# Issuing a round's loads ahead of the feed-forward stretch, and ordering the row halves of early chunks on TensorE itself

## The chip, the cores and the metric

One core of a Trainium2 chip runs the whole program. The metric is the device time of one execution in microseconds (us), the median of three executions. "PE" is TensorE's matmul stream, "PEld" its weight loads, "DVE" VectorE, "ACT" ScalarE, "POOL" GpSimd, and "SP" the engine whose queue issues nearly all transfers here.

## What is computed

A retention layer feeds a feed-forward layer with a squared ReLU:

```
scores = (q @ k.T) / sqrt(64)                 # q, k, v: 8 batches, 8 heads, 576 positions, 64 wide
attn   = (scores * gamma_h ** (i - j), i >= j) @ v
x      = attn as 4608 tokens x 512
out    = relu(x @ w_in) ** 2 @ w_out          # w_in 512 x 2048, w_out 2048 x 512
```

The decay is a power of a constant for each head, so it can be put into q and v by rows: q of position i is multiplied by gamma^i, v of position j by gamma^-j. What remains are plain products with a causal mask, and a running sum U = sum of k v^T that carries everything before the current piece.

## The kernel before

**Chunks.** Each batch of 576 positions is cut into chunks of 128, 128, 128, 128 and 64 positions, 40 chunks in all (`chunks`, `N_CH`). A chunk is worked in halves of 64 positions. For each half TensorE makes the scores (`score`, L449), which VectorE masks (`masked`, L461), the half's own contribution "own" (L480 or L568: masked scores times v), the growth of U, "grow" (L483 or L562), and the contribution of the past (L515 or L604: U times q). Own and past are added up in the same PSUM tile `x_ps`. All of these are products with 64 contraction rows: some use rows 0 to 63 of the array, some rows 64 to 127, and both kinds write the same places of `x_ps`. [...]

**How that order is made.** In the first ten chunks (`retain_a`, `retain_b`, `retain_c`), `retain_b` ends with a tiny ScalarE copy (L518, 128 x 2 elements of `x_ps` into a spare `u_sb`). It must wait for the products of `retain_b`, and the next products into `x_ps`, those of `retain_c`, must wait for it. The later chunks (`whole`) do without: their `wait_for` puts a no-operation on TensorE that waits for an earlier product's semaphore, and what shares a row half with the earlier products goes ahead of that wait.

**Rounds.** The main loop runs over i, 0 to 40. A round works chunk i - 1, prepares chunk i and then issues a stretch of the feed-forward layer (`ffn`). Up to i = 10 (`N_ONE`) a round is `retain_a`, some feed-forward work, `retain_b`, `scores`, `retain_c`, more feed-forward work. From i = 11 (`N_TURN`) on it is `whole(i - 1)` and then one stretch `ffn(i - 1, 2)`.

**Feed-forward.** The first layer goes over nine blocks of 512 tokens. Each block is four groups (`mp`) of seven products in a seven-product block scheme (`PRODUCTS`, `ffn_in`): a step is eight 128 x 128 x 256 matmuls (L708), and VectorE and ScalarE combine its result (L718 to L735) before the PSUM bank can be used again. The results g go out to a scratch tensor in DRAM (`g_sums`, store at L650). The second layer (L1038) reads them back after the attention part is over and runs to the end of the program.

**Loads and flips.** `load(i)` fetches q, k and v of a chunk: three transfers each for q and k, one for v. The pools `ld3`, `ld5` and `ld4` hold three q, five k and four v. q and k are needed transposed. Up to chunk 10 TensorE does that (`turn`); from chunk 11 on VectorE transposes blocks of 32 (`flip`, L396; k first, then q), and ScalarE moves them into place (`move`, L411). `flip(i + 2)` puts the two transposes into a list, and the stretch of feed-forward that follows takes one per step. q must first be scaled by POOL (`scale_q`, L375).

**Order.** Everything is written out by hand: `manual_schedule` keeps the program order on every engine, so on SP too transfers are issued strictly as the code names them, and one that has to wait holds back what is behind it. In the rounds up to 9 a round's loads fetch chunk i + 3. At i = 10 the loads turn to a longer lead: q and k of chunk 13, q and k of chunk 14, v of chunk 13; from there on q and k of chunk i + 4, v of chunk i + 3. All these loads stand at the end of the round (L921 to L929), behind its feed-forward stretch. The round i = 10 has one stretch more than the others, `ffn(i, 0)` at L918, ahead of its loads. The first flip of a chunk that was loaded at i = 10 is `flip(13)`, in the stretch of round 11.

Of the kernel before, what the change touches and what calls it, by code (L numbers as in the profile page):

```python
# [15 lines left out]
C = 128  # L16
CH = C // 2
# [23 lines left out]
def kernel(  # L41
# [315 lines left out]
    def rows(half, n=64):  # L357
        return slice(64 * half, 64 * half + n)
# [7 lines left out]
    def clears(half, bank):  # L366

        new = (half, bank) not in clean
        clean.add((half, bank))
        return new  # L370
# [100 lines left out]
    def x_at(hp, b, h):  # L471
        return xp[0][rows(b), hp // 2, 0:256].rearrange("p (g t) -> p g t", g=2)[:, hp % 2, CH * h:CH * h + CH]

    def within(i, h):

        s = st[i]
        b_, ci, c0, cs = chunks[i]
        own, grow = [], []
        for hp, e, b in HEADS:
            own.append(lambda hp=hp, e=e, b=b: nc.tensor.matmul(  # L480
                x_at(hp, b, h), lhsT=s["vs"][rows(h), 2 * hp + b, :], rhs=s["ret"][rows(h), e, hp, :],
                start=clears(b, hp // 2), stop=False, skip_group_check=True))
            grow.append(lambda hp=hp, e=e, b=b: nc.tensor.matmul(  # L483
                u_ps[0][rows(e), hp, :], lhsT=loaded[i][1][rows(1 - h), 2 * hp + e, :], rhs=s["vs"][rows(1 - h), 2 * hp + b, :],
                start=(ci == 0 and h == 1 and hp == 0), stop=(hp == HP - 1), skip_group_check=True))
        return own, grow
# [19 lines left out]
    def retain_b(i):  # L506

        s = st[i]
        b_, ci, c0, cs = chunks[i]
        for h in reversed(range(cs // CH)):  # L510
            if 2 * ci + h == 0:
                continue
            u = u_sb[(2 * ci + h) % 3]
            for hp, e, b in HEADS[0:2] + HEADS[4:6] + HEADS[2:4] + HEADS[6:8]:
                nc.tensor.matmul(x_at(hp, b, h), lhsT=u[rows(e), hp, :], rhs=s["qT"][rows(e), hp, CH * h:CH * h + CH],  # L515
                                 start=clears(b, hp // 2), stop=False, skip_group_check=True)

        nc.scalar.copy(u_sb[(2 * ci + (cs // CH)) % 3][:, 0:2, 0:1], xp[0][:, :, cs - CH:cs - CH + 1])  # L518

    def retain_c(i):  # L520

        b_, ci, c0, cs = chunks[i]
        own, grow = within(i, 0)
        more = ci + 1 < NCH
        for j in range(0, len(own), 2):
            for f in own[j:j + 2] + (grow[j:j + 2] if more else []):
                f()
        x_out(i, lambda: grown(i, 1) if more else None)

    def x_out(i, after):  # L530
# [20 lines left out]
                n_next[0] += 1  # L551
        st[i] = loaded[i] = None

    HEADS_1 = [(hp, e, e if hp < HP // 2 else 1 - e) for e in (1, 0) for hp in (0, 2, 1, 3)]

    def grow_of(i, h):

        ci = chunks[i][1]
        if ci == 0 and h == 0:
            u_ps[0] = ps_u.tile([128, HP, D], F32, tag="u", name="u_ps")  # L560
        u = u_ps[0]
        return [lambda hp=hp, e=e, b=b: nc.tensor.matmul(  # L562
            u[rows(e), hp, :], lhsT=loaded[i][1][rows(h), 2 * hp + e, :], rhs=st[i]["vs"][rows(h), 2 * hp + b, :],
            start=(ci == 0 and h == 0 and hp == 0), stop=(hp == HP - 1), skip_group_check=True) for hp, e, b in HEADS]

    def own_of(i, h):
        s = st[i]
        return [lambda hp=hp, e=e, b=b: nc.tensor.matmul(  # L568
            x_at(hp, b, h), lhsT=s["vs"][rows(h), 2 * hp + b, :], rhs=s["ret"][rows(h), e, hp, :],
            start=clears(b, hp // 2), stop=False, skip_group_check=True) for hp, e, b in HEADS_1]  # L570

    def wait_for(earlier):
        tc.add_manual_dep(nc.tensor.nop().ins, earlier.ins.name,
# [8 lines left out]
    def whole(i):  # L582

        b_, ci, c0, cs = chunks[i]
        s = st[i]
        xp[0] = ps_x.tile([128, 2, 256], F32, tag="x", name="x_ps", padded_shape=[128, 2, 512])
        clean.clear()
        more = ci + 1 < NCH
        out_of, into = own_of(i, 0), grow_of(i, 1) if more else []
        m = beside_each(out_of, into, (0, 2))[-1]  # L590
        beside_each(out_of, into, (4, 6))
        if more:
            grown(i, 1)
        if i + 1 < N_CH:
            scores(i + 1, True)
            score(i + 1, 0)
            score(i + 1, 1)
        wait_for(m)
        for h in range(cs // CH):
            if 2 * ci + h == 0:  # L600
                continue
            u = u_sb[(2 * ci + h) % 3]
            for hp, e, b in HEADS[0:2] + HEADS[4:6] + HEADS[2:4] + HEADS[6:8]:
                m = nc.tensor.matmul(x_at(hp, b, h), lhsT=u[rows(e), hp, :], rhs=s["qT"][rows(e), hp, CH * h:CH * h + CH],  # L604
                                     start=clears(b, hp // 2), stop=False, skip_group_check=True)
        grows = i + 1 < N_CH and chunks[i + 1][3] == C
        out_of, into = own_of(i, 1) if cs == C else [], grow_of(i + 1, 0) if grows else []
        beside_each(out_of, into, (0, 2))
        if i + 1 < N_CH:
            score(i + 1, 2)  # L610
            score(i + 1, 3)
            masked(i + 1)
        if cs == C:
            wait_for(m)
        beside_each(out_of, into, (4, 6))
        x_out(i, lambda: grown(i + 1, 0) if grows else None)
# [216 lines left out]
    def warm(count, wide):  # L833
        t = ps_f.tile([128, 512], F32, tag="f", name="idle_ps")
        for _ in range(count):
            if wide:
                nc.tensor.matmul(t[:, 0:128], lhsT=idle, rhs=idle, start=True, stop=True)
            else:
                for b in range(2):
                    nc.tensor.matmul(t[rows(b), 0:64], lhsT=idle[rows(0), rows(b)], rhs=idle[rows(0), 0:64], start=True, stop=True,  # L840
                                     skip_group_check=True)

    warm(6, True)
    scale_q(0, nc.vector)
    turn(0)
    for i in range(N_CH + 1):
        if i <= N_EARLY:

            if i == 1:
                convert(2)  # L850
            elif i == 2:
                convert(5)
            if i >= 1:
                retain_a(i - 1)
                if i < 3:
                    warm(4, False)
                elif i == N_EARLY:
                    turn(i)
                else:
                    convert(1)  # L860
                    first_in(1, (0,))
                    convert(5)
                retain_b(i - 1)
                if i < 3:
                    warm(4, False)
                retain_c(i - 1)
            convert((0, 1, 1, 0, 0)[i])
            if i == N_EARLY:
                fetch_raw(2)
                step()  # L870
            scores(i)
            if i == 2:
                convert(5)
                first_in(0, (0,))
            elif i == 3:
                convert(1)
                first_in(2, (0,))
                convert(3)
            elif i == N_EARLY:
                convert(3)  # L880
                step()
                convert(5)
            scale_q(i + 1, nc.gpsimd)
            if i < N_EARLY:
                if i < 2:
                    warm(6, False)
                if i + 1 < N_EARLY:
                    turn(i + 1)
        elif i > N_ONE:
            move(C, i)  # L890
            whole(i - 1)
            if i + 1 < N_CH:
                scale_v(i + 1)
            if N_TURN <= i + 2 < N_CH:
                flip(i + 2)
            ffn(i - 1, 2)
        else:
            if i == N_EARLY + 1:
                gone[0] = TOK
            retain_a(i - 1)  # L900
            if i < N_TURN:
                turn(i)
            move(C, i)
            ffn(i - 1, 0)
            retain_b(i - 1)
            if i < N_CH:
                scores(i)
            retain_c(i - 1)
            if i == N_ONE:
                scale_v(i + 1)  # L910
                for f in grow_of(i, 0):
                    f()
                grown(i, 0)
            if N_TURN <= i + 2 < N_CH:
                flip(i + 2)
            ffn(i - 1, 1)
            if i == N_ONE:
                ffn(i, 0)  # L918
        if i == 0:
            fetch_raw(2)  # L920
        if i < N_TURN - 1:  # L921
            load(i + 3)
        else:
            if i == N_TURN - 1:
                load(i + 3, "qk")
            if i + 4 < N_CH:
                load(i + 4, "qk")
            if i + 3 < N_CH:
                load(i + 3, "v")  # L929
        if 0 < i < N_EARLY:  # L930
            fetch_raw(1)
        if i == N_ONE - 1:
            scale_v(i + 1)
        if i > N_EARLY:
            for j in range(n_scaled[0], min(i + (4 if i > N_TURN - 4 else 3), N_CH)):
                n_scaled[0] += 1
                scale_q(j, nc.gpsimd)
# [251 lines left out]
```

## Time and profile before

| | us |
|---|---|
| three executions | 973.71, 975.15, 977.31 |
| median | 975.15 |
| span of the profiled execution, first to last instruction | 975.6 |
| PE busy in the span | 952.2 |
| DVE busy | 783.0 |
| ACT busy | 338.4 |
| POOL busy | 127.7 |
| DMA queue 1, share of 16 engines | 58.1% |

The profiled execution is the one that took 977.31 us. A busy share says how long at least one instruction of an engine was under way. Three stages can be told by the profile: up to about 118 us the early chunks, the conversion of w_in and the first block of the feed-forward layer; from there to about 522 us the `whole` rounds with the first layer; then the end of the first layer and the second layer. From 600 us on PE and its weight loads are busy all the time (100.00 of each 100 us).

### The profile page before, as it was taken

To read this page: it belongs to the slowest core of one execution; us is meant where nothing else is said; L and a number is where in the kernel's file an instruction comes from. 1 tells how busy PE (TensorE), PEld (TensorE's weight loads), DVE (VectorE), ACT (ScalarE), POOL (GpSimd) and SP (SyncE) were. 2 spreads that over 40 slices of the span, in tenths; PEclk is the share of its full clock that TensorE was granted. 3 is DMA by queue.
4 is the path that set the end of the run, shared out by engine and by line. 5 is a ranking of instruction groups with operands and counts; after the bars stand their busy time and mean duration, and the time that the engine had idled before them with its cause. 6 is when DMAs were issued, how large, how long until landed. Compare 5 with 4: busy or idle time off the path is not lost. (4 is left out here: it accounts for less than half of the span.)

```text
span 975.6 us, 24006 instructions
## 1 busy us (share of the span) xinstructions
PE 952.2 (98%) x10108; PEld 856.3 (88%) x10108; DVE 783.0 (80%) x1447; ACT 338.4 (35%) x818; POOL 127.7 (13%) x121
## 2 busy tenths in 40 slices
PE   7799989999999999999999999999999999999998
PEld 6654668888887888888888889999999999999998
DVE  4789769988988779888866587888888787787876
ACT  3445356765664865676730100000000000000000
POOL 3221222222312222222210000000000000000000
PEclk9999999999999999999999999999999999999999
DMA  9875636686666766785367967545353454524241
GB/s 203 234 211 141 189 99 184 159 246 217 180 183 215 207 174 175 226 238 155 111 232 294 355 250 253 199 158 184 109 205 131 166 192 178 201 109 173 88 173 44
DMA packets 172013, 181.43 MB, mean 186 GB/s; under 512 B 118145, under 2 KB 132481, under 8 KB 165249
## 3 DMA queue, kind: packets, MB, share of 16 engines
q1 hardware_dynamic: 169792, 179.38, 58.1%
q8 instruction: 79, 1.29, 0.5%
q10 hardware_dynamic: 2112, 0.52, 0.2%
q14 instruction: 30, 0.24, 0.1%
HBM read 109.36 MB, written 70.52 MB: 184 GB/s over the span
## 5 line engine op out<-in xcount | busy, mean ns | idle before, releaser
L708 PE MATMUL h_b<-room,w 128*128 128x256 f32 x768 | 183.9, 382 | 3.0 <-DVE room L635 1.9
L411 ACT COPY qk<-flip 32x256 f32<-32x256 f32 x416 | 167.4, 402 | 8.5 <-DVE flip L396 2.3
L708 PEld LDWEIGHTS h_b<-room,w 128*128 128x128 f32 x768 | 144.7, 191 | 25.0 <-issue 2.2
L1038 PE MATMUL o_b<-w,room 128*128 128x128 f32 x1168 | 144.4, 275 | 0.2 <-DVE room L990 0.2
L1038 PEld LDWEIGHTS o_b<-w,room 128*128 128x128 f32 x1168 | 137.3, 192 | 0.4 <-DVE room L990 0.4
L708 PE MATMUL h_c<-room,w 128*128 128x256 f32 x512 | 122.7, 383 | 3.8 <-DVE room L722 3.8
L1038 PE MATMUL o_c<-w,room 128*128 128x128 f32 x1008 | 123.0, 275 | 0.0
L708 PE MATMUL h_a<-room,w 128*128 128x256 f32 x512 | 122.0, 381 | 0.0
L1038 PEld LDWEIGHTS o_c<-w,room 128*128 128x128 f32 x1008 | 117.7, 192 | 0.0
L708 PEld LDWEIGHTS h_c<-room,w 128*128 128x128 f32 x512 | 96.9, 191 | 17.6 <-DVE room L722 4.2
L708 PEld LDWEIGHTS h_a<-room,w 128*128 128x128 f32 x512 | 96.5, 190 | 14.1 <-issue 0.5
L1052 ACT COPY r<-o_a 128x128 f32<-128x128 f32 x53 | 14.1, 265 | 271.7 <-PE o_a L1038 236.0
L1038 PE MATMUL o_a<-w,a 128*128 128x128 f32 x688 | 85.6, 275 | 0.0
L1038 PEld LDWEIGHTS o_a<-w,a 128*128 128x128 f32 x688 | 81.2, 192 | 0.1
L725 POOL TENSOR_TENSOR room<-room 128x512 f32<-128x512 f32 x32 | 34.9, 1092 | 306.4 <-ACT room L724 306.4
L715 DVE SCALAR_TENSOR_TENSOR room<-room 128x512 f32<-128x512 f32 x96 | 70.2, 731 | 3.3
L672 PE MATMUL h_ps<-room,w 128*128 128x512 f32 (+1 forms) x152 | 59.8, 541 | 2.7 <-DVE w L228 1.8
L375 POOL TENSOR_TENSOR q_ld<-q_ld,dv 128x512 f32<-128x512 f32 (+1 forms) x39 | 44.9, 1151 | 116.3 <-DMA q_ld<-in_q_dram 112.0
L727 DVE TENSOR_TENSOR room<-h_b,room 128x512 f32<-128x512 f32 x32 | 22.0, 689 | 38.9 <-PE h_b L708 38.9
L468 POOL TENSOR_TENSOR v_ld<-v_ld,dv 128x512 f32<-128x512 f32 (+1 forms) x40 | 48.3, 1209 | 23.5 <-DMA v_ld<-in_v_dram 13.9
L672 PEld LDWEIGHTS h_ps<-room,w 128*128 128x128 f32 x152 | 28.0, 192 | 25.9 <-issue 22.4
L1038 PE MATMUL o_b<-w,a 128*128 128x128 f32 x344 | 45.4, 275 | 0.0
(110 smaller groups left out, 1391.2 us busy)
## 6 DMA issues: line engine op xcount, KB each, us to landing
g_dram<-room SPq DMA_DIRECT2D x32, 1280.0 KB, 5.7
a<-g_dram SPq DMA_DIRECT2D x30, 1024.0 KB, 6.2
room<-g_dram SPq DMA_DIRECT2D x15, 1024.0 KB, 6.0
w<-w_dram SPq DMA_DIRECT2D x7, 1792.0 KB, 10.5
out_dram<-room SPq DMA_DIRECT2D x17, 512.0 KB, 3.3
w<-in_moe_w_in_dram SPq DMA_DIRECT2D x16, 512.0 KB, 6.3
w<-in_moe_w_out_dram SPq DMA_DIRECT2D x16, 512.0 KB, 4.5
v_ld<-in_v_dram SPq DMA_DIRECT2D x31, 256.0 KB, 3.9
```

Source lines behind the costliest of these rows:

```text
L375: engine.tensor_tensor(t, t, dv[:cs, :, NCH + ci:NCH + ci + 1].to_broadcast([cs, H, D]), op=ALU.mult)
L411: nc.scalar.copy(*moves.pop(0)[2:])
L468: nc.gpsimd.tensor_tensor(vs[:cs], vs[:cs], dv[:cs, :, ci:ci + 1].to_broadcast([cs, H, D]), op=ALU.mult)
L672: nc.tensor.matmul(p.rearrange("p h t -> p (h t)"), lhsT=w[:, c, :], rhs=xT[0][:, c, lo * HT:hi * HT], start=(c == 0), stop=(c == N_DM - 1))
L708: nc.tensor.matmul(p[:, mm, :], lhsT=w[:, c, :], rhs=xs[n][right][:, c, :], start=(j in OPENS and mm == 0 and c == 0), stop=(j in CLOSES a ...
L715: nc.vector.scalar_tensor_tensor(t, t, 0.0, t, op0=ALU.max, op1=ALU.mult)
L725: nc.gpsimd.tensor_tensor(g["A11"], g["A11"], g["A11"], op=ALU.mult)
L727: nc.vector.tensor_tensor(g["A22"], p, p15, op=ALU.add)
L1038: nc.tensor.matmul(p, lhsT=s["lefts"][left][:, m, :], rhs=w_out[j][:, m, WO_SLOT[right], :], start=(i in OPENS and m == 0), stop=(i in CLO ...
L1052: nc.scalar.copy(r[:, 0, 0:128], p)
```

## The change

There are two edits. The first moves the loads: a function `loads(i)` holds what stood at the end of the round. From round 11 on it is called right behind `whole(i - 1)` and `scale_v`, in front of the feed-forward stretch; in round 10 it stays behind `ffn(i - 1, 1)` but is now in front of `ffn(i, 0)`; in the earlier rounds it stays where it was. The purpose is that transfers start as soon as the chunk's products have freed the buffers, not behind the stores and waits of a stretch of feed-forward.

The second edit takes the ScalarE copy L518 out of `retain_b`. `retain_c` keeps the same products but in another order: first the "own" products on the row half that was last used for the same places, then a no-operation on TensorE that waits for the last product of `retain_b`, then the others. `own_of` gets an argument for which half comes first; for `whole` it makes the same order as before. The purpose is to order the row halves on TensorE alone.

```
 def retain_b(i):
...
-                nc.tensor.matmul(x_at(hp, b, h), lhsT=u[rows(e), hp, :], rhs=s["qT"][rows(e), hp, CH * h:CH * h + CH],
-                                 start=clears(b, hp // 2), stop=False, skip_group_check=True)
-
-        nc.scalar.copy(u_sb[(2 * ci + (cs // CH)) % 3][:, 0:2, 0:1], xp[0][:, :, cs - CH:cs - CH + 1])
+                s["read"] = nc.tensor.matmul(
+                    x_at(hp, b, h), lhsT=u[rows(e), hp, :], rhs=s["qT"][rows(e), hp, CH * h:CH * h + CH],
+                    start=clears(b, hp // 2), stop=False, skip_group_check=True)
 
     def retain_c(i):
 
         b_, ci, c0, cs = chunks[i]
-        own, grow = within(i, 0)
         more = ci + 1 < NCH
-        for j in range(0, len(own), 2):
-            for f in own[j:j + 2] + (grow[j:j + 2] if more else []):
-                f()
+        own, grow = own_of(i, 0, 0), grow_of(i, 1) if more else []
+        beside_each(own, grow, (0, 2))
+        wait_for(st[i]["read"])
+        beside_each(own, grow, (4, 6))
         x_out(i, lambda: grown(i, 1) if more else None)
...
+    def loads(i):
+        if i < N_TURN - 1:
+            load(i + 3)
+            return
+        if i == N_TURN - 1:
+            load(i + 3, "qk")
+        if i + 4 < N_CH:
+            load(i + 4, "qk")
+        if i + 3 < N_CH:
+            load(i + 3, "v")
...
             whole(i - 1)
             if i + 1 < N_CH:
                 scale_v(i + 1)
+            loads(i)
             if N_TURN <= i + 2 < N_CH:
                 flip(i + 2)
             ffn(i - 1, 2)
...
             ffn(i - 1, 1)
-            if i == N_ONE:
-                ffn(i, 0)
         if i == 0:
             fetch_raw(2)
-        if i < N_TURN - 1:
-            load(i + 3)
-        else:
-            if i == N_TURN - 1:
-                load(i + 3, "qk")
-            if i + 4 < N_CH:
-                load(i + 4, "qk")
-            if i + 3 < N_CH:
-                load(i + 3, "v")
+        if i <= N_ONE:
+            loads(i)
         if 0 < i < N_EARLY:
             fetch_raw(1)
+        if i == N_ONE:
+            ffn(i, 0)
```

More of the change, by code (lines that the diff above doesn't have):

```diff
@@ L552, in x_out @@
         st[i] = loaded[i] = None
-    HEADS_1 = [(hp, e, e if hp < HP // 2 else 1 - e) for e in (1, 0) for hp in (0, 2, 1, 3)]
     def grow_of(i, h):
@@ L564, in grow_of, with own_of @@
             start=(ci == 0 and h == 0 and hp == 0), stop=(hp == HP - 1), skip_group_check=True) for hp, e, b in HEADS]
-    def own_of(i, h):
+    def own_of(i, h, first):
         s = st[i]
@@ L569, in own_of @@
             x_at(hp, b, h), lhsT=s["vs"][rows(h), 2 * hp + b, :], rhs=s["ret"][rows(h), e, hp, :],
-            start=clears(b, hp // 2), stop=False, skip_group_check=True) for hp, e, b in HEADS_1]
+            start=clears(b, hp // 2), stop=False, skip_group_check=True)
+            for e in (first, 1 - first) for hp, e_, b in (HEADS[j] for j in (e, e + 4, e + 2, e + 6))]
     def wait_for(earlier):
@@ L588, in whole @@
         more = ci + 1 < NCH
-        out_of, into = own_of(i, 0), grow_of(i, 1) if more else []
+        out_of, into = own_of(i, 0, 1), grow_of(i, 1) if more else []
         m = beside_each(out_of, into, (0, 2))[-1]
@@ L606, in whole @@
         grows = i + 1 < N_CH and chunks[i + 1][3] == C
-        out_of, into = own_of(i, 1) if cs == C else [], grow_of(i + 1, 0) if grows else []
+        out_of, into = own_of(i, 1, 1) if cs == C else [], grow_of(i + 1, 0) if grows else []
         beside_each(out_of, into, (0, 2))
```

## The prediction

> **What bounds the kernel now.** I read the busy shares first, then TensorE's waits, then, at the largest wait, the stretch around it in order of time.
>
> ```profile
> PE 952.2 (98%) x10108; PEld 856.3 (88%) x10108; DVE 783.0 (80%) x1447; ACT 338.4 (35%) x818; POOL 127.7 (13%) x121
> ```
>
> TensorE is busy for 952.2 of 975.6 us, so no more than 23.4 us of idle time can be won, apart from time in which it runs at a lower clock. Added up by tens of us, 10.9 of these idle us lie before 50 us, where weights are still being fetched and converted, and 3.2 in the last 15.6 us. What lies behind 118 us is small, and the list of TensorE's waits from 118 to 530 us names it (waited for, us in total, times, longest); the lines of VectorE over the same stretch and of SyncE's queue over the whole span belong to it:
>
> ```profile
> PE h_c L708 <- DVE room L722: 3.8, 1, 3.8
> PE h_b L708 <- DVE room L635: 1.9, 1, 1.9
> PE h_b L708 <- DVE room L727: 0.9, 2, 0.5
> ```
> ```profile
> DVE flip L396 <- DMA k_ld<-in_k_dram: 7.2, 1, 7.2
> ```
> ```profile
> SPq L650 <- DVE room L649: 163.1, 25, 12.1
> ```
>
> One wait of 3.8 us is the largest single item, and VectorE has one wait for a transfer, 7.2 us, for the k of a flip. Are they the same event? The timeline from 100 to 150 us says so (start, duration, engine, line):
>
> ```profile
> 116.68 1.14 SPq L196 DMA_DIRECT2D w<-in_moe_w_out_dram  x2
> 127.80 0.38 SPq L650 DMA_DIRECT2D g_dram<-room  x1
> 128.23 0.52 SPq L148 DMA_DIRECT2D q_ld<-in_q_dram  x1
> 128.80 2.53 SPq L150 DMA_DIRECT2D q_ld<-in_q_dram  x2
> 131.37 0.57 SPq L148 DMA_DIRECT2D k_ld<-in_k_dram  x1
> 131.99 1.49 SPq L150 DMA_DIRECT2D k_ld<-in_k_dram  x2
> ```
> ```profile
> 137.94 0.71 DVE L396 STREAM_TRANSPOSE flip<-k_ld 128x512 f32<-128x512 f32 x1 [7.25 <-DMA k_ld<-in_k_dram]
> 138.58 0.65 DVE L722 TENSOR_TENSOR room<-h_c,room 128x512 f32<-128x512 f32 x1
> ```
> ```profile
> 133.60 1.89 PE L708 MATMUL h_b<-room,w 128*128 128x256 f32 x8
> 139.28 2.84 PE L708 MATMUL h_c<-room,w 128*128 128x256 f32 x8 [3.79 <-DVE room L722]
> 142.51 2.56 PE L708 MATMUL h_b<-room,w 128*128 128x256 f32 x8 [0.38 <-DVE room L727]
> ```
>
> The queue has nothing to issue from 117.82 (116.68 + 1.14) to 127.80: the next entry is the store L650, which waits for L649. Behind it stand the loads of round 10, k of chunk 13 among them. They are issued at 131.37 to 133.48, `flip(13)` wants that k at 130.69 (end of L461) and gets it at 137.94. VectorE stands still, L722 is queued behind the flip and frees h_c's bank, so TensorE stands still for 3.79 us.
>
> The idle time also costs clock. The answer by single microseconds (length, PE, PEld, DVE, ACT, POOL busy with counts, granted clock, DMA share, GB/s):
>
> ```profile
> 140.00:141.00 1.00, 1.00 (x4) 0.84 (x4) 1.00 (x3) 0.00 (x0) 1.00 (x1) 0.64 0.98 220
> 141.00:142.00 1.00, 1.00 (x3) 0.34 (x1) 1.00 (x3) 0.00 (x0) 0.30 (x1) 0.50 0.04 7
> 142.00:143.00 1.00, 0.62 (x2) 0.49 (x2) 0.97 (x2) 0.00 (x0) 0.96 (x1) 0.50 0.00 0
> 143.00:144.00 1.00, 1.00 (x4) 0.80 (x4) 1.00 (x2) 0.00 (x0) 0.09 (x1) 0.65 0.00 0
> ```
>
> The clock is down for about 3.4 us; the missing shares are 0.36 + 0.50 + 0.50 + 0.35 = 1.71 us.
>
> [...]
>
> **The change part by part.**
>
> *Round 10's loads ahead of `ffn(10, 0)`.* In the new order of SP they stand right behind the two L196 issues, ahead of the store. They can start at 117.82. q of 13 needs the buffer of q of 10, last read by `turn(10)` (about 115.2); k of 13 that of k of 8, long free; q of 14 that of q of 11, flipped at 110.72. q before k costs 3.1 us of issue in the old trace (128.23 to 131.33), k 2.1 us, so k of 13 is issued by about 123.1; with the median 3.8 us from issue to landing it is there by 127, 3.7 us ahead of 130.69. q of 13 lands by about 126, POOL scales it in 1.06 us, and its flip comes only at the second step. So the wait of 7.25 us goes, and with it 3.79 + 0.38 = 4.17 us of TensorE and the 1.71 us of clock: **5.9 us**. A cross-check: from the h_b at 133.60 to the next chunk's products at 148.45 are 14.85 us for five steps; at the 1.72 us from step to step that stand around it (131.88 to 133.60) they would take 8.6, which makes 6.2. Does VectorE bind in its place? From 130.00 to the end of L649 at 149.11 it worked 19.1 - 7.25 = 11.9 us, and TensorE needs 130.04 to about 142.5, 12.5 us, for the same stretch: close, but no more than some 0.3 us of waits.
>
> *Later rounds' loads ahead of the stretch.* They come some 15 us earlier, but no flip waits for a transfer there, so nothing is won. What is now behind them on SP: stores L650, raw weights L196, stores of w_out's sums. A round's seven issues took 152.69 to 156.83, 4.1 us, at its densest. That is the most by which these can be late. The queue waited 163.1 us for VectorE ahead of L650 and so comes early; g's room is used again two groups later, 14 steps of 1.72 us or 24 us, against 5.7 us to landing; the raw weight fetched at 152.30 is at least 20 us ahead of its use. I take 0, hidden by that lead; the bounds are 0 and 0.4 us a round.
>
> *L518 out.* Ten copies of 0.16 us on ScalarE, which is 35% busy: nothing. What counts is the round trip PE, ACT, PE. With scores in between it is nearly hidden:
>
> ```profile
> 117.37 0.65 PE L449 MATMUL sc_ps<-qk 64*64 64x64 f32 x32
> 117.69 0.16 ACT L518 COPY u_sb<-x_ps 128x2 f32<-128x2 f32 x1
> ...
> 117.96 0.57 PEld L480 LDWEIGHTS x_ps<-qk,v_ld 64*64 64x64 f32 x16
> ```
>
> L518 ends at 117.85, and L480 starts behind it, as the scores are nearly through: 0.05 to 0.1 us for each of six chunks, about 0.3 us. Chunks 2 and 3 have no scores there; TensorE idles 0.28 us each and could start up to 0.5 us earlier, but soon VectorE waits 1.79 us for raw w_in at 44.47, which the edit doesn't move. I take 0 of at most 1.0.
>
> *The new wait on TensorE.* Behind it are four "own" and four "grow" products and then all of TensorE's work, so any latency would count. In `whole` the same wait stands behind the last L604, and around 129.3 to 129.7 no idle row shows. Eight products or sixteen scores cover it. Bounds 0 and 0.2 us for each of ten; I take 0.
>
> Sum for the profiled execution: 5.9 + 0.3 = 6.2 us. It took 977.31, the longest of three; the median is 2.2 us shorter, and I can't see whether the drop of the clock was in it. Without it the gain is 4.2 + 0.3 = 4.5, with it 6.2. Between the two, 5.4: **969.7 us**.
>
> **The rivals.** *VectorE binds instead.* Its margin in the repaired stretch is 0.6 us of 12.5, and an order of flips that comes earlier could meet the weights' conversion. For it: VectorE is busy 7.86 of 8 us from 142 to 150. Against it: much of that is catching up. Half of the 4.2 us comes back, the drop of clock goes or was not there: 975.15 - 2.1 - 0.3, **972.7**.
>
> *Stores and weights come late, slower than before.* 29 rounds in which the loads hold SP ahead of what the feed-forward steps need; at the upper bound of 0.4 us a round this costs 11.6 us against the gain of 5.4: 975.15 + 6.2, **981.4**. Against it: VectorE waited for no w_out transfer at all.
>
> *More than the stall.* The early chunks pass on 1.0 us, and the other drop of the clock, slices of 0.91 and 0.92 from 40 to 60 us behind an idle 2.1 us, is missed in turn: 969.7 - 1.0 - 1.7, **967.0**.
>
> **How the numbers follow.** The forecast has 0.68, "VectorE binds" 0.15, "slower" 0.06, "more" 0.11. The range of 967.0 to 973.5 holds the forecast, VectorE's case and half of "more", and leaves out the slower one. Faster by over 0.5% means below 970.27: the forecast lies only 0.6 us below, so about 0.78 of its chance falls there, 0.53, and "more" adds 0.11: 0.64. The rest of the forecast, 0.15, and VectorE's 0.15 are no change: 0.30. Slower: 0.06.
>
> **What would show it.** In the new profile SP issues q and k of round 10 from about 118 us, ahead of the store at about 128; the wait of the flip for k is gone; TensorE's wait for L722 is gone; the clock has no drop near 140; L518 and its waits are gone, and the no-operation in `retain_c` leaves no idle rows. The prediction is wrong if the flip still waits, if VectorE or TensorE waits for raw weights or g's room in the later rounds, or if the drop of clock shows elsewhere.

## The result, and the profile after

The changed kernel took 968.32 us (median of four executions, 967.80 to 969.81) against 974.43 us for the kernel before on the same chip: a ratio of 0.9935, with an interval of 0.9910 to 0.9961. Measured again later it took 967.56 us against 974.57, a ratio of 0.9937 (0.9921 to 0.9954). The gain is 6 to 7 us.

Line numbers of the changed kernel are one lower around the feed-forward steps: its L707, L719, L721, L726, L634, L648 and L649 are L708, L720, L722, L727, L635, L649 and L650 of the kernel before; its L560 and L566 are L562 and L568.

The page's first part for the changed kernel (busy us, share of the span, instructions):

```profile
PE 948.8 (98%) x10108; PEld 854.6 (88%) x10108; DVE 781.3 (81%) x1447; ACT 337.0 (35%) x808; POOL 129.8 (13%) x121
```

Here it is the span that counts: 966.4 us instead of 975.6, so TensorE is idle for 17.6 us instead of 23.4, 5.8 us less. ScalarE has ten instructions fewer; those are the ten copies L518. Which idle time went, the list of TensorE's waits from 110 to 530 us of the changed kernel tells (waiting operation, what it waited for, us in total, times, longest):

```profile
PE h_b L707 <- DVE room L634: 1.9, 1, 1.9
PE sc_ps L449 <- ACT qk L411: 0.7, 1, 0.7
PE h_b L707 <- DVE room L726: 0.5, 1, 0.5
PE u_ps L560 <- issue: 0.5, 1, 0.5
PE h_b L707 <- DVE room L719: 0.2, 1, 0.2
```

The wait of h_c for VectorE's L721 (3.8 us before) is no longer in it. With it went 0.4 us of waiting at the next bank (L727 before, L726 here), and the line marked "issue" is 0.3 us shorter; the other lines differ by 0.1 us at most. In all the list is 4.4 us shorter; the rest of the 5.8 us lies ahead of 110 us. The timeline of SyncE's queue in the changed kernel (start, duration, engine, line, transfer) shows why:

```profile
114.00 1.08 SPq L196 DMA_DIRECT2D w<-in_moe_w_out_dram  x2
115.18 0.38 SPq L148 DMA_DIRECT2D q_ld<-in_q_dram  x1
115.61 1.24 SPq L150 DMA_DIRECT2D q_ld<-in_q_dram  x2
116.89 0.48 SPq L148 DMA_DIRECT2D k_ld<-in_k_dram  x1
117.42 1.09 SPq L150 DMA_DIRECT2D k_ld<-in_k_dram  x2
118.92 2.12 SPq L148 DMA_DIRECT2D q_ld<-in_q_dram  x1
...
126.49 0.37 SPq L649 DMA_DIRECT2D g_dram<-room  x1
```

q and k of chunk 13 come right behind the two raw weights, ahead of the store of 126.49; k is issued by 118.51. VectorE, from the timeline of the changed kernel (a bracket at the end would be idle time just before, and what released it):

```profile
127.92 0.68 DVE L461 TENSOR_TENSOR qk<-sc_ps,msk 128x512 f32<-128x512 f32 x1
128.52 0.70 DVE L396 STREAM_TRANSPOSE flip<-k_ld 128x512 f32<-128x512 f32 x1
129.18 0.69 DVE L721 TENSOR_TENSOR room<-h_c,room 128x512 f32<-128x512 f32 x1
...
130.39 0.70 DVE L396 STREAM_TRANSPOSE flip<-q_ld 128x512 f32<-128x512 f32 x1
```

No bracket stands on either flip: k was issued ten us ahead of its flip, and L721 follows at once. TensorE over the next stretches, by ten microseconds (length; busy us and count of PE, PEld, DVE, ACT, POOL; granted clock; DMA share; GB/s):

```profile
130.00:140.00 10.00, 10.00 (x81) 8.58 (x83) 8.93 (x15) 7.86 (x18) 3.57 (x3) 1.00 0.45 106
140.00:150.00 10.00, 10.00 (x144) 8.94 (x135) 9.93 (x15) 8.37 (x21) 3.82 (x3) 1.00 0.94 260
```

PE is busy for all of it and the clock stays at 1.00.

**The spans differ by more than the gain.** 975.6 - 966.4 is 9.2 us. Counted from the first step of the feed-forward layer that stands on h_a (start 109.25 us in the kernel before, 106.55 in the changed one), the rest of the span is 866.3 and 859.8 us: 6.5 us apart. The other 2.7 us lie in the early stage. It is tempting to credit them to the second edit, which acts there; the experiments below don't bear that out.

### The profile page after: what moved, and what is told of

It is laid out like the page before. It is cut to its first block, busy times and chain, and to the rows that moved or that the text cites. A ratio compares the mean times of both kernels' runs of the same rounds, so it can differ in the third digit from the quotient of the medians.

```text
span 966.4 us, 24021 instructions
## 1 busy us (share of the span) xinstructions
PE 948.8 (98%) x10108; PEld 854.6 (88%) x10108; DVE 781.3 (81%) x1447; ACT 337.0 (35%) x808; POOL 129.8 (13%) x121
## 5 line engine op out<-in xcount | busy, mean ns | idle before, releaser
L707 PE MATMUL h_b<-room,w 128*128 128x256 f32 x768 | 183.4, 382 | 2.6 <-DVE room L634 1.9
L411 ACT COPY qk<-flip 32x256 f32<-32x256 f32 x416 | 167.4, 402 | 8.4 <-DVE flip L396 2.3
L707 PEld LDWEIGHTS h_b<-room,w 128*128 128x128 f32 x768 | 144.3, 190 | 24.1 <-issue 2.2
L707 PE MATMUL h_a<-room,w 128*128 128x256 f32 x512 | 122.0, 381 | 0.0
L707 PE MATMUL h_c<-room,w 128*128 128x256 f32 x512 | 121.8, 381 | 0.0
L707 PEld LDWEIGHTS h_a<-room,w 128*128 128x128 f32 x512 | 96.5, 190 | 14.1 <-issue 0.5
L707 PEld LDWEIGHTS h_c<-room,w 128*128 128x128 f32 x512 | 96.6, 190 | 13.4
L714 DVE SCALAR_TENSOR_TENSOR room<-room 128x512 f32<-128x512 f32 x96 | 72.5, 756 | 3.3
L468 POOL TENSOR_TENSOR v_ld<-v_ld,dv 128x512 f32<-128x512 f32 (+1 forms) x40 | 51.2, 1281 | 14.0 <-DMA v_ld<-in_v_dram 7.8
L726 DVE TENSOR_TENSOR room<-h_b,room 128x512 f32<-128x512 f32 x32 | 22.0, 689 | 37.8 <-PE h_b L707 37.8
L566 PE MATMUL x_ps<-qk,v_ld 64*64 64x64 f32 x1024 | 49.6, 224 | 0.0
```

Of the source, the lines that this page charges most:

```text
L411: nc.scalar.copy(*moves.pop(0)[2:])
L468: nc.gpsimd.tensor_tensor(vs[:cs], vs[:cs], dv[:cs, :, ci:ci + 1].to_broadcast([cs, H, D]), op=ALU.mult)
L566: return [lambda hp=hp, e=e, b=b: nc.tensor.matmul(x_at(hp, b, h), lhsT=s["vs"][rows(h), 2 * hp + b, :], rhs=s["ret"][rows(h), e, hp, :], ...
L707: nc.tensor.matmul(p[:, mm, :], lhsT=w[:, c, :], rhs=xs[n][right][:, c, :], start=(j in OPENS and mm == 0 and c == 0), stop=(j in CLOSES a ...
L714: nc.vector.scalar_tensor_tensor(t, t, 0.0, t, op0=ALU.max, op1=ALU.mult)
L726: nc.vector.tensor_tensor(g["A22"], p, p15, op=ALU.add)
```

## The experiments

The theory: round 10's loads alone make the gain, because SyncE's queue stood at a store that waited; the second edit and the later rounds' loads are worth nothing that shows. The rivals: that part of it comes from the second edit (the early stage's 2.7 us), or from the later rounds.

**Taking the change apart.** Four kernels, each with one part of the diff on the kernel before.

*Loads alone*: `loads(i)` in both places, retain_b and retain_c as before.

> The kernel before with the first edit alone: loads moved in round 10 and in all later rounds, L518 kept. Theory A (the queue's head in round 10 held back the loads, all of the gain comes from that): VectorE's wait of 7.2 us and TensorE's wait of 3.8 us are gone, time 969.0, 0.994 of before. Theory B (the order on TensorE saves 2.9 us of the early chunks, as the span up to 116 us seems to show): this kernel wins only the other 5.5 us minus what the clock's drop does by chance, about 971.5, 0.997 of before.

*Order alone*: L518 out, the wait on TensorE in; loads as before.

> The kernel before with the second edit alone: L518 gone, TensorE's own wait in the early chunks, loads as before. Theory A: no measurable change, 974.1 (0.3 us less), the waits of 7.2 us and 3.8 us still there. Theory B: 971.5, and the step that started at 119.07 us before starts some 2.9 us earlier.

*Only round 10's loads*, and *only the later rounds' loads*:

```
 (round 10 alone)                          (later rounds alone)
-            if i == N_ONE:                             scale_v(i + 1)
-                ffn(i, 0)                 +            loads(i)
...                                        ...
         loads(i)                          +        if i <= N_ONE:
+        if i == N_ONE:                    +            loads(i)
+            ffn(i, 0)                     (round 10 still behind ffn(i, 0))
```

> The kernel before with round 10's loads alone moved ahead of its second stretch of feed-forward; the later rounds load at their end as before, L518 kept. Theory A: all of the gain, 969.0, 0.994 of before, the flip's wait gone. Theory C (the gain comes from loads that are ahead in each of the later rounds): 973.5 or more, with the later rounds still to be won.

> The kernel before with the loads of the rounds from 11 on moved ahead of the feed-forward stretch and round 10 left as it was. Theory A: no gain, 974.4, flip's wait of about 7 us and TensorE's of about 3.8 us still there. Theory C: most of the gain, about 970. If loads ahead of stores and weights cost anything, it is seen here alone: 0.4 us a round would make 986.

| | us | ratio to before | interval | from the first h_a step to the end, us | clock near 140 us |
|---|---|---|---|---|---|
| before | 974.4 to 974.8 | | | 866.3 | drops |
| both edits | 968.32, 967.56 | 0.9935, 0.9937 | 0.9910 to 0.9961, 0.9921 to 0.9954 | 859.8, 860.2 | 1.00 |
| loads alone | 969.20 | 0.9952 | 0.9938 to 0.9966 | 860.1 | 1.00 |
| order alone | 974.23 | 0.9997 | 0.9988 to 1.0006 | 867.8 | drops |
| round 10's loads alone | 967.86 | 0.9935 | 0.9921 to 0.9949 | 860.4 | 1.00 |
| later rounds' loads alone | 974.56 | 0.9997 | 0.9982 to 1.0011 | 866.2 | drops |

The first h_a step starts at 104.77 to 106.55 us in the profiles of the kernels without L518 and at 105.21 to 109.25 in those with it: the two ranges overlap, and the kernel with round 10's loads alone, L518 still in, has 105.89, earlier than the changed kernel's 106.55. So the early stage moves by some us from one execution to the next, the second edit is worth something between a gain of 1.2 us and a loss of 0.6 (0.9988 and 1.0006 of 974.5), and the column behind that step is the one to read: 866 to 868 us with the stall, about 860 without it.

**The parts, step by step.** Behind the first h_a step the profiles repeat each other closely, so that small effects can be told apart which the times leave open:

- The stall. From the first h_a step to the step of h_c behind the next chunk (150.59 us in the kernel before) it is 41.34 us before, and 35.35 with all loads alone, 35.36 with round 10's loads alone: 6.0 us.
- The second edit. The step that starts at 119.07 us before, behind the last chunk that has L518, follows the one at 115.17 by 3.90 or 3.91 us in every profile of a kernel with L518, and by 3.71 or 3.72 in every one without: 0.2 us.
- The later rounds' loads. Where they come early, the stretch from 150.59 to 166.85 us is 16.49 to 16.51 us long, else 16.25 or 16.26; but the step at 270.66 us follows the one before it by 4.44 to 4.46 us, else 5.05 to 5.09. That is 0.2 us lost and 0.6 won, some 0.4 us in all. What holds the step there was not looked into.

6.0 + 0.2 + 0.4 is 6.6 us for the changed kernel, and 6.5 were measured. So the stall is not quite the whole gain, but nine tenths of it.

The waits show the same. TensorE's line for the wait in question, order alone:

```profile
PE h_c L707 <- DVE room L721: 3.4, 1, 3.4
```

Later rounds' loads alone, with its windows by 20 us (columns as above), where the clock of 0.93 and 0.99 means 0.07 x 20 + 0.01 x 20 = 1.6 us at full speed lost:

```profile
PE h_c L708 <- DVE room L722: 3.4, 1, 3.4
```
```profile
120.00:140.00 20.00, 16.50 (x172) 13.35 (x170) 12.33 (x20) 12.96 (x31) 4.98 (x5) 0.93 0.55 138
140.00:160.00 20.00, 20.00 (x208) 17.20 (x208) 19.83 (x30) 11.44 (x26) 5.53 (x4) 0.99 0.55 147
```

With round 10's loads alone that line is gone, and so is VectorE's wait of 7.2 us. The only wait for a k that its list still has is that of an earlier flip, at 116.00 us:

```profile
DVE flip L396 <- DMA k_ld<-in_k_dram: 0.6, 1, 0.6
```

**Is it the store at the head of the queue?** That the loads come earlier when they are written earlier doesn't yet say what held them. So the loads stay behind the stretch, and only the store at which the queue stood (that of the first group of the second block) goes to another engine's queue, ScalarE's:

```
-  lambda: nc.sync.dma_start(g_dram[n, ...
+  lambda: (nc.scalar if (n, mp) == (1, 0) else nc.sync).dma_start(g_dram[n, ...
```

> The kernel before with one transfer on another queue: the first store of g of the second block, the one that stood ahead of round 10's loads, is issued by ScalarE; SP's order is otherwise that of before, and the loads stay behind the stretch in the program. Theory A (the waiting store at the head of the queue held back the loads, nothing else did): SP starts round 10's loads some ten us earlier, at about 118, the flip's wait goes, time 968.5 to 969.5. Rival D (the loads could not have started earlier, for buffers or because of where they stand in the program): the wait stays at about 7 us, 974.4.

It took 972.49 us, 0.9978 of before (0.9970 to 0.9986): a gain of 2.3 us, less than half of what was expected. SyncE does begin the loads early, and the flip's wait is gone. But ScalarE now stands at the store (timelines of this kernel, SyncE's and ScalarE's queue; then TensorE's wait and its windows of one us, columns as above):

```profile
116.91 0.39 SPq L148 DMA_DIRECT2D q_ld<-in_q_dram  x1
```
```profile
128.45 0.38 ACTq L650 DMA_DIRECT2D g_dram<-room  x1
128.87 1.65 ACT L411 COPY qk<-flip 32x256 f32<-32x256 f32 x4 [2.88 <-DVE w L210]
```
```profile
PE sc_ps L449 <- ACT qk L411: 3.3, 4, 1.9
```
```profile
128.00:129.00 1.00, 0.00 (x0) 0.00 (x0) 1.00 (x3) 0.13 (x1) 0.00 (x0) 1.00 0.69 159
129.00:130.00 1.00, 0.26 (x2) 0.19 (x2) 0.95 (x2) 0.96 (x3) 0.00 (x0) 0.96 1.08 338
130.00:131.00 1.00, 0.50 (x16) 0.43 (x18) 0.00 (x0) 0.88 (x3) 0.00 (x0) 0.50 1.03 387
```

Behind the store on ScalarE stand the moves L411 that the next scores need. ScalarE is idle for 2.88 us ahead of them, TensorE has nothing to do from 128 to 129 us, and half clock follows, to 136.7 us in this profile. The wait wasn't removed, it changed its engine. (The profiled execution was the slowest of the sixteen, 976.44 us, so its length isn't typical; the wait and where it stands are what it is read for.)

So the same store was given to an engine that has nothing urgent behind it, GpSimd:

```
-  lambda: nc.sync.dma_start(g_dram[n, ...
+  lambda: (nc.gpsimd if (n, mp) == (1, 0) else nc.sync).dma_start(g_dram[n, ...
```

> The kernel before, with one edit: the first 32-column store of round 10, the one that SyncE's queue stood at, is issued by GpSimd in place of SyncE; loads stay behind the stretch. Theory (what stalls is a queue in order whose head waits; GpSimd has nothing urgent behind that store): SyncE begins the round's loads at about 117, k is there before the flip of 128, the flip's wait of 7 us is gone, no wait of the scores for ScalarE comes in its place, 968.5 to 969.5 us. Rival (the wait moves with the store, as it did on ScalarE): scale_q of chunk 13, behind the store on GpSimd, comes late, the flip of q waits for it 1 to 4 us, and the time is 970.5 to 972.5.

It took 968.02 us, 0.9939 of before (0.9922 to 0.9956), with the loads where they were in the kernel before: the whole gain of the change. In this kernel's timeline SyncE goes on to the loads, GpSimd waits at the store and still scales q of chunk 13 ahead of its flip, and neither flip of chunk 13 has a bracket:

```profile
116.75 0.38 SPq L148 DMA_DIRECT2D q_ld<-in_q_dram  x1
```
```profile
126.63 1.03 POOL L650 DMA_DIRECT2D g_dram<-room  x1 [6.76 <-DVE room L649]
127.68 1.59 POOL L375 TENSOR_TENSOR q_ld<-q_ld,dv 128x512 f32<-128x512 f32 x1
```
```profile
129.17 0.70 DVE L396 STREAM_TRANSPOSE flip<-k_ld 128x512 f32<-128x512 f32 x1
...
131.84 0.70 DVE L396 STREAM_TRANSPOSE flip<-q_ld 128x512 f32<-128x512 f32 x1
```

The scaling ends at 129.27, the flip of q starts at 131.84. So what stalled the kernel before is the store at the head of SyncE's queue, which waited there from 117.82 to 127.80 us, not the distance of the loads in the code and not the transfer time.

**Is it enough to have k come first?** The flip waited for k, and q was issued ahead of k. In this kernel the loads and the store stay, and only k and q of chunk 13 change places:

```
-                load(i + 3, "qk")
+                load(i + 3, "k")
+                load(i + 3, "q")
```

> The kernel before with k of chunk 13 issued ahead of its q, still behind the store. Theory A: k lands some 3 us earlier, the flip's wait for k falls from 7 to about 4 us, but the second flip then waits for q and for POOL, so a new wait of about 2.5 us takes its place; TensorE idles some 3 us in two pieces. [...]1.7 us are won beside the 1 us of idle time: 972; if the clock drops all the same, 973.5. Rival E (k alone matters): TensorE's idle time there falls under 1 us, 969.5.

It took 974.55 us, 0.9998 of before (0.9989 to 1.0006): no gain, against 1.5 to 2.5 us expected. The timelines of this kernel, SyncE, VectorE and TensorE:

```profile
124.84 0.38 SPq L650 DMA_DIRECT2D g_dram<-room  x1
125.27 0.52 SPq L148 DMA_DIRECT2D k_ld<-in_k_dram  x1
125.84 2.53 SPq L150 DMA_DIRECT2D k_ld<-in_k_dram  x2
```
```profile
133.57 0.71 DVE L396 STREAM_TRANSPOSE flip<-k_ld 128x512 f32<-128x512 f32 x1 [5.83 <-DMA k_ld<-in_k_dram]
134.20 0.65 DVE L722 TENSOR_TENSOR room<-h_c,room 128x512 f32<-128x512 f32 x1
134.78 1.49 DVE L239 TENSOR_TENSOR w<-w 128x512 f32<-128x512 f32 x1
```
```profile
134.91 1.99 PE L708 MATMUL h_c<-room,w 128*128 128x256 f32 x8 [2.38 <-DVE room L722]
138.39 1.99 PE L708 MATMUL h_b<-room,w 128*128 128x256 f32 x8 [1.48 <-DVE room L727]
...
145.74 0.38 PE L449 MATMUL sc_ps<-qk 64*64 64x64 f32 x9 [0.52 <-ACT qk L411]
```

Two things ate it. The slow issue of 2.53 us belongs to the place behind the store, not to q: now k has it, so k is out 3.5 us after the store (124.84 to 128.37) instead of 5.7, and the flip's wait falls only from 7.25 to 5.83 us. And what TensorE no longer waits for at L722 it waits for further on, at L727: 2.38 + 1.48 + 0.39 us (L731, the third line of that kind) is 4.25, against 3.79 + 0.38 = 4.17 before. Behind the late flip VectorE works without a pause in both kernels, and it is VectorE that TensorE catches up with. In the kernel before a good part of that was hidden, because TensorE ran at half clock for 3.41 us there (140.28 to 143.69); here the clock stayed at 1.00, and the same lag shows as idle time.

VectorE was slower besides. From the flip of k to L210, on whose result ScalarE waits before it can go on to the moves L411, it took 9.52 us (133.57 to 143.09) against 7.88 before (137.94 to 145.82): L239, L241 and L214 took 1.49, 1.54 and 1.28 us against 1.23, 0.68 and 0.41. The last line above, 0.52 us for a move L411 ahead of the next scores, comes of it. So the pause ahead of h_c is 1.41 us shorter, but from h_c to the step of h_c behind the next chunk it takes 12.61 us (134.91 to 147.52) against 11.31 (139.28 to 150.59), and from the first h_a step to the end it is 866.3 us in both.

GpSimd was busy without a pause from 134.66 to 141.55 beside VectorE. In the five cases seen beside GpSimd L241 took 1.54 us (134.16 and 148.65 us in the changed kernel, 139.10 with k first, 141.80 with the store on ScalarE, 135.61 with the store on GpSimd), and 0.68 or 0.69 us in the six cases of the kernel before and the changed one without GpSimd at work beside it. Why the two go together, and whether L239 and L214 are slow for the same reason, the traces don't say. No run here took GpSimd's work away and left the rest, so this is seen side by side, not tried.

**The next wait.** With the stall gone, the 1.9 us for L634 head the list of TensorE's waits. TensorE and VectorE in the changed kernel:

```profile
286.61 1.97 PE L707 MATMUL h_b<-room,w 128*128 128x256 f32 x8 [1.87 <-DVE room L634]
```
```profile
285.78 0.68 DVE L634 TENSOR_TENSOR room<-room 128x512 f32<-128x512 f32 x1
```

L634 is a sum that the second step of the next block of 512 tokens needs. Such sums are taken one per step behind the steps 3, 4 and 5 of the last group before the block, if the block's last tokens are there; here they were there only in time for step 5. So one sum (L633) was taken, and L634 came behind all of step 6's work. The edit on top of the changed kernel takes a second sum at step 5 when three are left:

```
             sums_x[n + 1].pop(0)()
+            if j == 5 and len(sums_x[n + 1]) == 3:
+                sums_x[n + 1].pop(0)()
```

> The kernel after with one more edit, at what is now TensorE's longest wait in the attention rounds, 1.9 us for the second sum of x of a block that has just been completed: that sum is taken one step earlier on VectorE when only one was taken so far. If VectorE's order is what makes it wait, the 1.9 us fall to 0.6 and the time to about 967.2, a gain of 0.13% that the interval may not show; if VectorE's load is the limit, the wait moves to the next step and nothing is won.

> The changed kernel with the first chunk's sum of a block taken one step sooner in the feed-forward stretch, again, beside the changed kernel on one chip. If the wait of TensorE of 1.9 us that it takes away is worth its length: 966.4 us. If the lower time seen of it earlier was scatter of the chip: 968.3.

It took 965.20 us (0.9903 of before, 0.9890 to 0.9916) and, beside the changed kernel on one chip, 965.15 against 967.56 (0.9905, 0.9885 to 0.9925, against 0.9937, 0.9921 to 0.9954): 2.4 us by the medians. The two intervals touch, but each of the eight executions with the second sum (at most 965.74 us) was shorter than each of the ten without it (at least 967.04). The two profiled spans differ by 2.0 us (963.9 and 965.9), about the length of the wait, which went wholly and not down to 0.6 us. In the edited kernel's timeline L634 comes 2.4 us sooner, counted from the first h_a step (105.96 us here, 106.55 in the changed kernel), ahead of the flip, and the step starts without idle time:

```profile
282.79 0.69 DVE L634 TENSOR_TENSOR room<-room 128x512 f32<-128x512 f32 x1
```
```profile
283.99 1.89 PE L707 MATMUL h_b<-room,w 128*128 128x256 f32 x8
```

For the changed kernel on that chip, the expectation was:

> The changed kernel unaltered, to have it on the same chip as the next one: 968.3 us, 0.9935 of the kernel before.

## Why the prediction was right, point by point

*Round 10's loads.* Right in mechanism and order. The queue issued q and k of chunk 13 from 115.18 on, right behind the raw weights. k was out 3.3 us after q began (115.18 to 118.51) where the prediction counted 5.2 us by the old trace: the slow issue of 2.53 us, which it took for q's own, doesn't occur there (one of 2.12 us does at 118.92, behind k). An error to the safe side: k is issued ten us ahead of its flip.

*Its size, 5.9 us in the profiled execution.* 866.3 - 859.8 = 6.5 us between the two profiles; with round 10's loads alone it is 866.3 - 860.4 = 5.9, with all loads alone 866.3 - 860.1 = 6.2. Both of the prediction's ways of counting, 5.9 by waits and clock and 6.2 by steps, lie there; the stall by itself is 6.0 (above).

*From 5.9 + 0.3 to 5.4 for the median.* This is the term that was mis-sized. The prediction could not see whether the drop of the clock was in the median execution too, and took the middle of 4.5 and 6.2. The profiles with the stall (before, order alone, later rounds alone) have the drop behind it; those of the repaired kernels have none there. Over all executions on record the mean clock was 0.9959 in the kernel before (67 executions, in three series) and 0.9978 in the kernels without the stall (27 in five series): 1.9 us of full clock apart. So on the whole the stall costs clock too, but four of the 67 executions show 1.000, so the drop isn't in every one.

What was wrong is the case without the drop. The prediction takes all of the 1.71 us off there, as if slow clock and VectorE's lag added up, but they overlap. In the kernel before VectorE ends L727 at 142.45 us, and the step that waits for it, at 142.51, could have started no sooner at full clock. Behind it the slow clock still costs 0.7 us: that step takes 2.40 us (142.51 to 144.91) in place of 1.72. So without the drop the stall would cost about 6.0 - 0.7 = 5.3 us, not 4.2; this is an estimate from one profile. The kernel with k first agrees: its clock doesn't drop, and it waits 1.48 us at L727 instead of 0.38. The measured gains are 6.1 and 7.0 us for the change, 6.6 for round 10's loads alone, 6.6 for the store on GpSimd and 5.3 for all loads alone.

975.15 - 6.2 is 969.0. What is left between 969.7 and 968.32 is thus that term (0.8 us) and a median of before that was 0.7 us lower in the comparison (974.43) than in the three executions at hand (975.15).

*The later rounds' loads: 0.* Right for the time: 0.9997, with an interval that leaves room for a gain of 1.8 or a loss of 1.1 us over 29 rounds, far from the 11.6 us of the slower rival; the 0.4 us that the steps show lies inside it. The prediction took 4.1 us for the most by which the loads can hold up what is behind them. That was a quick round: the seven issues of the next one in the same profile, right behind a store, last from 164.49 to 172.61, 8.1 us. The lead of the stores and weights covered that too. The list of SyncE's waits for the changed kernel shows that the stores still come early and wait for VectorE:

```profile
SPq L649 <- DVE room L648: 154.8, 24, 12.1
```

That is 8.3 us less than the 163.1 before. The one store of round 10 accounts for it: it waited from 117.82 to 127.80 before, 10.0 us, and waits from 124.97 (end of the last load) to 126.49 now, 1.5.

*L518 out: 0.3 us.* Not seen in the time: order alone is 0.9997, and 0.3 us lies inside its interval. The steps show it at one place, 0.2 us at the last chunk with the copy, where the prediction had 0.05 to 0.1 us; what the earlier chunks give is lost in the scatter ahead of the first h_a step. The copy itself is gone, and where TensorE stood for it the next products follow (below).

*The new wait on TensorE: 0.* Right, with a number. In the early chunk whose row halves are changed at 36.9 us of the changed kernel, the timeline of TensorE is:

```profile
36.87 0.22 PE L566 MATMUL x_ps<-qk,v_ld 64*64 64x64 f32 x1
36.88 0.22 PE L560 MATMUL u_ps<-v_ld,k_ld 64*64 64x64 f32 x1
36.95 0.27 PE L566 MATMUL x_ps<-qk,v_ld 64*64 64x64 f32 x2
```

The no-operation stands between 36.88 and 36.95: a spacing of 0.07 us, and one of 0.11 behind it, where the pairs around follow each other by 0.05 to 0.06. In the kernel before 0.28 us of idle time stood there for L518. The time doesn't show that difference. Both kernels put an order between the two row halves, by L518 or by this wait; that one is needed at all was not shown, as no run went without.

*VectorE binds instead: no.* From 118 to 142 us TensorE is busy for 24.00 of 24.00 us and VectorE for 22.48, so its margin was about as thin as the prediction said (1.5 us of 24, against 0.6 of 12.5), and it held. The one experiment in which VectorE did take over is the one with k first, where it started the same work 5.8 us late.

*More than the stall: no.* The last early chunk passed on 0.2 us; the 2.7 us ahead of it are within the scatter of that stage. An early drop of the clock wasn't missed either: in the changed kernel's profile it stands between 20 and 30 us (0.83 there).

## What to carry to other kernels

A wait of one engine for a transfer is first read backwards: when was it issued, and what stood at the head of that queue before it? If that is an instruction which itself waits for late work, loads go in front of it (967.86 us here, against 974.5), or it goes to a queue that has nothing urgent behind (968.02); moved to an engine with urgent work behind it, it takes its wait along (972.49). When a repair shifts only part of the delay, look one buffer further: TensorE's idle time came back at the next bank (1.48 us at L727 with k first, against 0.38 before). Before a slow clock is added to an idle time, see whether another engine's lag would have held TensorE up anyway (here some 0.7 us of the 1.71 us of clock is left by itself, by the estimate above). And before crediting a profile's difference to an edit, count from an event behind the noisy stage (9.2 us of span became 6.5).

## What the runs showed of the hardware that was not expected

**The length of a pause doesn't settle whether the clock drops.** Behind the pauses of 3.4 to 3.8 us it dropped in all three profiles (before, order alone, later rounds alone). But behind 2.1 us in the early stage of the kernel before (46 to 48 us) and behind some 1.9 us with the store on ScalarE (127.8 to 129.74 us) it dropped too, and behind 2.38 us with k first it didn't. Nor is the time at half clock fixed: 3.4 us in the kernel before, but 6.8 with the order alone (135.5 to 142.3) and with the store on ScalarE.

In the kernel before the clock falls at 48.12 and at 140.28 us and stays at 0.50 for 3.41 us each time; the two drops are 92.16 us apart, 27 times that. In the changed kernel the one stretch at half clock, from 22.97 us, is as long, and the 6.8 us above are twice as long. In the 3.41 us ahead of the drops that follow the pauses near 130 to 140 us TensorE was busy for 0.29 (before), 0.37 (order alone) and 0.44 of the time (store on ScalarE). So the stretch ahead of a drop wasn't wholly idle. Nor does its busy share give a limit: a stretch of 0.47 in the early stage (changed kernel from 19.56 us) was followed by a drop, and one of 0.45 in the kernel before (from 293.88 us, 45 times 3.41 us behind the drop at 140.28) wasn't. With k first the 3.41 us from the start of the pause (132.53 us) were busy for 0.30, and no drop followed. That the place of the pause on steps of 3.41 us counts as well is the author's estimate, from the 27 steps between the two drops and from the 0.30 without one; no run here varied the place alone.

**Transfers right behind a store were slow to issue, whatever they fetched**: 2.53 us for two of q in the kernel before, and 2.53 us for two of k with k first; in the changed kernel two of q took 2.93 us at 127.49. Where some 3 us lay between the store and the loads (140.60 and 144.16 us in the changed kernel), the pair took 1.04. But a store isn't needed: with six loads ahead of it and no store, a single transfer of q took 2.12 us at 118.92 in the changed kernel and 2.32 at 120.42 with the store on GpSimd, while the pairs around took 1.02 to 1.36. What makes these places slow was not tried.
